# Eight output rows in one block, and single maxima in every step: a two-branch attention kernel

## The chip, the core and the metric

The kernel runs on one core of a Trainium2 chip. The metric is the device time of one execution in microseconds (us); a kernel's time is the median of its runs. The core's engines are TensorE (PE, with its weight loads PEld), VectorE (DVE), ScalarE (ACT), GpSimd (POOL) and SyncE (SP, which here only issues transfers). They run at the same time, each through its own list of instructions in order, and wait for each other by semaphores. Matmul results land in PSUM banks, which ACT and DVE read.

## The reference

Two attention branches over the same 2048 x 512 input are mixed by a gate:

```python
x = A_x
g = _sigmoid((x * gate_w).sum(-1, keepdims=True))
a = _A_ref(x, A_wqkv, A_wo)      # 32 heads of 16; each position attends to 8 earlier ones, 2 apart
b = _B_ref(x, B_wq, B_wk, B_wv, B_wo)  # 32 query heads of 16 on one key/value head, full softmax
return g * a + (1 - g) * b
```

Branch B is `softmax(q k^T / 4) v` over all 2048 keys for every one of the 32 heads, then a 512 x 512 output projection. Branch A's softmax has 8 terms a position, then its own output projection. All data is float32.

## The kernel before, in words

**Units and steps.** Branch B is cut into 32 units: 4 blocks of 512 queries by 8 groups of 4 heads (`NU`). A unit has 16 steps, one for each tile of 128 keys, so there are 512 steps (`NS`). A step s does two things on PE: `exp_pair` (L468) makes the scores of two pairs of heads in the PSUM banks `pe` (the two buffers `eb`), which ACT turns into exponentials `pexp` (L475, 128x1024 each, two a step); `weighted` (L480) multiplies the previous step's exponentials by the values and adds them into bank `po` (L483; four matmuls, eight in the profile's count). When a unit is over, `finish_a` (L495) has DVE transpose `po` (L497), after which the next unit may overwrite `po`; DVE and POOL then divide and shape the result.

**Maxima.** The softmax needs a maximum for each query and head before the exponentials of a unit start. The kernel therefore computes all scores twice: once, ahead of time, only for the maxima. A maximum task is one 62x512 matmul on one half of the array, reduced by DVE. There are 2048 of them, 64 a unit. They come in these ways:

- `fill_pair` (L339): two matmuls, one on each half of the array, into the two-bank tile `pm` (the variable `m2`); one DVE reduction (L344).
- `fill_one` (L348): one matmul into the one-bank tile `ps` (the variable `m1`), a "single"; one DVE reduction (L355).
- `fill_diff` and `fill_sum` (L411, L424): two key tiles at a time by half sums and half differences; ACT takes absolute values (L419), DVE adds and reduces (L429). Only inside the streams named below.
- `pause` (L863): when a unit's maxima would come too late, pairs are made on `pm` and on the score banks `pe`, with nothing beside them.

When the last maximum of a unit is made, `filled` (L329) has DVE reduce and transpose them, POOL splits them, and eight small transfers (L461) write them into two rows of the unit's query tile `qst`, so that the scores come out shifted. Query tiles are loaded by `stack` (L286) some units ahead; there are eight.

**The front.** `stream` (L689) makes the projections of x, matmul by matmul in halves of the array, and puts maxima beside them. It ends with the last projection in bank `pm`; near its end the list `ended` stops new pairs on `pm` (L716, L1068).

**Output rows.** The output is 16 rows of 128 positions (`NJ`). Each needs both branches' projections, three products each (high and low parts). Rows 0 to 11 are made by `out_phase` (L728), a block of four rows between two steps that again is a `stream`: output matmuls in halves (L740), row turning on PE (L646), maxima beside them. Rows 12 to 15 can only be begun when the last units are done. `spread` (L776) lays them between the last steps, up to a few matmuls at a time into `pm` (L812), with `turn_all` (L783, ACT copy L786) and `prepare` (ACT copy L637, POOL subtraction L639) for the next row; the part of the last two units (the fourth product group) is added at the very end (L1163 to L1188).

**What sets the order.** The program is a fixed list for each engine, made when it is built by the loop over steps (L1106 to L1155). That loop keeps clocks of its own (`clk`, `free`) with estimated durations, and decides with them in every step: whether an output block stands there (L1130), whether a pair is made (`fill_ready`, L853) and whether a single is made, which it is while `singles` (L849) finds more maxima left than later pairs and rows will take. `order` says in which sequence of the two score pairs, the pair and the single a step emits. Slow estimates or fast ones change the list, not the waiting on the chip.

Of the kernel before, what the change touches and what calls it, by code (L numbers as in the profile page):

```python
# [6 lines left out]
F32 = mybir.dt.float32  # L7
F32R = mybir.dt.float32r
AF = mybir.ActivationFunctionType
# [9 lines left out]
NJ = S // P  # L19
# [29 lines left out]
def gated_mix_kernel(ctx, tc, xt, wa, wk, wq, wo_a, wo_b, out):  # L49
# [36 lines left out]
    def after(eng, ready, dur):  # L86
        clk[eng] = max(clk[eng], ready) + dur
        return clk[eng]
# [219 lines left out]
        return bool(half) or bool(slots) and slots[0][0] < len(stacked) and stacked[slots[0][0]] <= clk["pe"]  # L308

    def unit_tile(v):  # L310
        for x in (v, v + 1) if pe else (v,):
            if x < NU and x not in left:
                mx[x] = wp.tile([P, 2, 2, 4, 4], F32, name="mx", bufs=3)
                if pe:
                    nc.gpsimd.memset(mx[x], -FMAX)
                    charge(250)
                else:
                    nc.scalar.activation(mx[x].rearrange("p b i t k -> p (b i t k)"), ident[:, 0:64], AF.Identity, scale=0.0, bias=mk[:, 6:7])
                left[x] = NF // NU
        return mx[v]  # L320
# [5 lines left out]
    def to_go():  # L326
        return 2 * len(slots) + len(half)
# [448 lines left out]
    def spread(js, n):  # L776

        m = 3 * (C + n)

        def turn_all(j):  # L780
            bank = m1
            for c in range(C):
                nc.tensor.transpose(bank[:, c * P:(c + 1) * P], oa[c // 2][:, j, c % 2 * P:(c % 2 + 1) * P], ident)  # L783
            after("pe", 0, 0.7)
            own = p2[0].tile([P, C, P], F32, name="raw", bufs=1)
            nc.scalar.activation(own, bank.rearrange("p (c q) -> p c q", c=C), AF.Copy)  # L786
            after("act", clk["pe"] + T_LAT, 0.6)
            return own

        def parts_a(j, own):  # L790
            nonlocal pool
            hi, lo = turned[j, 0] = [pe[0].tile([P, C, P], F32R, name=f"turned{x}", bufs=1) for x in range(2)]
            nc.scalar.activation(hi, own, AF.Copy)
            at = after("act", clk["pe"], 0.6)
            nc.gpsimd.tensor_sub(lo, own, hi.bitcast(F32))
            pool = max(pool, 1e3 * at) + 1300

        prepare(js[0], n)
        yield 1.0
        parts_a(js[0], turn_all(js[0]))  # L800
        yield 3.0
        while slots or half:
            yield 1.0
        for j in js:
            nxt = j + 1 if j != js[-1] else None
            items = []
            for i in range(m):
                items = items or out_items(j, n)
                st, mv = items[i]
                for b in range(2):  # L810
                    h = slice(64 * b, 64 * b + 64)
                    nc.tensor.matmul(m2[:, b, :], st()[h], mv[h], start=(i == 0), stop=(i == m - 1))  # L812
                after("pe", 0, T_R)
                row_left[0] = m - 1 - i
                if i == 3 * n and nxt:
                    prepare(nxt, n)
                if i == m - 8 and nxt:
                    raw = turn_all(nxt)
                if i < m - 1:
                    yield 0.0  # L820
            del turned[j, 0], turned[j, 1]
            x = len(parts)
            if x < 2:
                spare.append(p2[0].tile([P, 512], F32, name="part", tag=("own", "tr8")[x], bufs=1))
            elif x == 2:
                two = p2[0].tile([P, 2, 512], F32, name="part", tag="pr", bufs=1)
                spare.extend([two[:, 0, :], two[:, 1, :]])
            parts[j] = spare[x]
            nc.scalar.activation(parts[j], m2[:, 1, :], AF.Copy)
            after("dve", after("act", clk["pe"] + T_LAT, 0.5), 0.7)  # L830
            nc.vector.tensor_add(parts[j], m2[:, 0, :], parts[j])
            if nxt:
                parts_a(nxt, raw)
            yield 1.5
        done.add("last")

    def spread_some(k):
# [11 lines left out]
    def singles(s):  # L849

        return 2 * max(0, 16 * (NU - 1) - 16 - s) + PER_ROW * max(0, NJ - 4 - outs) < to_go()
# [208 lines left out]
    def done_mm(at):  # L1060
        nonlocal pool
        x, i = at
        lump = lumps[x]
        if i % 3 == 2:
            run_tasks()
            if p2:
                run_pool()
        if x == last - 1 and i == 3 * C - 2:  # L1068
            ended.add(1)
        if x == last and i in (2, 7):  # L1070
            exp_pair(0, int(i == 2))
        if i < 3 * C - 1:
            return
        if lump[0] == "q":
            m = lump[1]
            queries_post(m, eb[x % 2])
            free[f"e{x % 2}"] = clk["act"]
            ahead_wa(0, m - 4)
        else:
            gg, j = lump[1:]  # L1080
            a_post(gg, j, 2 if x == last else x % 2)
            if gg + 1 < C:
                ahead_wa(gg + 1, j - 2)
# [22 lines left out]
    for s in range(NS + 1):  # L1106
        u, kt = divmod(s, NJ)
        if s == 16 * NB + 4:
            half_back()
        if len(stacked) < NU and s > 16 * (home(len(stacked))[1] + 1):  # L1110
            stack(len(stacked))
        if s < NS and kt == 0 and u not in shifted:
            while u not in shifted:
                clk["pe"] += 0.5
                run_tasks()
                if u not in shifted and left.get(u, 1):
                    assert pause(4)
        v = min(x[0][0] for x in (half, slots, [(NU,)]) if x)
        need = left.get(v, NF // NU)
        steps = 16 * v - 6 - s  # L1120
        short = need - 2.8 * max(0, steps) if v < NU else 0
        lead = (NF - to_go()) / 64 - s / 16
        order = (0, "m2", "m1", 1) if s > 1 else (1, "m2", 0, "m1") if s else ()
        k, n = outs // 4, C - (outs >= NJ - 4)
        if outs == NJ - 4:
            if NU - 3 in shaped and not half and not singles(s) and not later_rows and "last" not in done:
                later_rows.append(spread(list(range(outs, NJ)), n))
            if short > 0 and steps < 2:
                pause(short)
        elif due or outs < NJ and s and kt == 0 and outs // NH in done and NHG * (k + 1) - 1 in shaped and (lead < LEAD or s >= 16 * (NHG * (k + 2) + 1)):  # L1130
            if not due:
                prepare(outs, n)
                due.append(n)
            else:
                out_phase(list(range(outs, outs + 4)), due.pop(), kt == 1)
                outs += 4
                order = (0, "m1", 2)
        elif short > 0 and steps < 2:
            pause(short)

        for which in order:
            if which == "m2":
                fill_ready("m2", M2S)
            elif which == "m1":
                if not later_rows and (kt or not s) and singles(s):
                    fill_ready("m1", M1S)
            elif s < NS:
                exp_pair(s, which % 2 or which // 2, which == 2)
        spread_some(4)
        if s:  # L1150
            weighted(s - 1)
            if kt == 0 and s < NS:
                finish_a(u - 1, nc.gpsimd)
        run_tasks()
        run_pool()  # L1155
# [10 lines left out]
    for x in range(2):  # L1166
        js = slice(2 * x, 2 * x + 2)
        two = pe[0].tile([P, 2, 256], F32, name="ttl", tag="tt", bufs=2)
        tt, own = two[:, 0].rearrange("p (b d) -> p b d", d=32), two[:, 1]
        nc.vector.transpose(two[:, 0], po[:, 256 * x:256 * x + 256])  # L1170
        rl = wp.tile([P, 8], F32, name="rll", tag="rl", bufs=2)
        nc.vector.reciprocal(rl, tt[:, :, 16])
        nc.vector.tensor_mul(rl, rl, gate_t[:, NQB - 1, js].rearrange("p j b -> p (j b)"))
        nc.vector.tensor_mul(obp["t"][:, 8 * x:8 * x + 8, 1, :], tt[:, :, 0:DH], rl.unsqueeze(2).to_broadcast([P, 8, DH]))
        nc.vector.transpose(own, obp["t"][:, 8 * x:8 * x + 8].rearrange("p b h d -> p (b h d)"))
        tl = wp.tile([P, 2, 256], F32R, name=f"tl{x}", tag="aext", bufs=2)
        nc.scalar.activation(tl[:, 0], own, AF.Copy)
        nc.gpsimd.tensor_sub(tl[:, 1], own, tl[:, 0].bitcast(F32))
        tls.append(tl)
    for x in range(2):  # L1180
        for k, w in ((0, woh), (0, wol), (1, woh)):
            for t in range(2):
# [35 lines left out]
```

## Time and profile before

| | |
|---|---|
| median of 3 runs | 1504.08 us (1503.17 to 1506.13) |
| profiled execution | 1503.76 us, its span 1502.0 us |
| granted PE clock, mean | 0.997 |
| scores and exponentials: ACT L475 | 1021 x 1.02 us |
| weighted matmuls: PE L483 | 4096, 0.61 us each, up to eight overlapped |
| pairs: DVE L344 | 508 x 1.22 us |
| singles: DVE L355 | 446 x 0.68 us |

In the profile's rows a line like L344 is the line of the kernel, `out<-in` are tile names, `x8` is a count of merged instructions, and a bracket at the end gives the idle time of that engine before it and what ended it. Rows of the timeline begin with the start in us from the span's start and then the time from the first start to the last end. Rows of a table by windows give the window, its length, then the busy time and count of PE, PEld, DVE, ACT and POOL, the granted PE clock, and the share and rate of the transfers.

### The profile page before, as it was taken

How to read it: one execution, taken by the hardware profiler on the slowest of the kernel's cores; microseconds unless marked ns; L12 is line 12 of the kernel's file. 1: busy time of each engine (PE TensorE's matmuls, PEld its weight loads, DVE VectorE, ACT ScalarE, POOL GpSimd, SP SyncE). 2: the span in 40 equal slices, each digit the busy share in tenths (PEclk: the TensorE clock that was granted, in tenths of full speed). 3: DMA queues.
4: the chain of work that ended last, by engine and by line, in shares of the span. 5: the costliest groups of instructions: out<-in, count | busy, mean ns of one | idle time of the engine just before them, and what ended most of it. 6: DMA issues, size and time to landing. Idle time of an engine off the chain costs nothing.

```text
span 1502.0 us, 29449 instructions
## 1 busy us (share of the span) xinstructions
PE 1479.2 (98%) x11020; PEld 710.5 (47%) x11020; DVE 1188.4 (79%) x1814; ACT 1285.7 (86%) x1672; POOL 1024.8 (68%) x1806
## 2 busy tenths in 40 slices
PE   9999999999999999999999999999999999999998
PEld 6899888433333333333733345333333463333343
DVE  6976666788888888888788888888888888888801
ACT  5568988899999999999899988999989889999785
POOL 7876988788888888988988799788897130111021
PEclk9999999999999999999999999999999999999999
DMA  6754223121120211211212112021120000000000
GB/s 219 212 147 143 76 87 117 33 83 46 60 84 12 73 58 41 70 41 41 69 41 70 41 41 87 12 70 41 41 76 16 12 30 12 2 1 2 1 2 28
DMA packets 44287, 87.75 MB, mean 58 GB/s; under 512 B 9520, under 2 KB 25952, under 8 KB 39920
## 3 DMA queue, kind: packets, MB, share of 16 engines
q1 hardware_dynamic: 37136, 46.89, 10.3%
q0 software_dynamic: 6432, 37.94, 7.5%
q8 instruction: 86, 1.41, 0.4%
q10 hardware_dynamic: 576, 1.05, 0.2%
q14 instruction: 57, 0.47, 0.1%
HBM read 59.02 MB, written 26.30 MB: 57 GB/s over the span
## 4 chain that ended last, share of the span: by engine, by line
PE 91%; ACT 5%; DVE 2%; issue 1%; DMA 0%; POOL 0%; SPq 0%; DVEq 0%; ACTq 0%; POOLq 0%
PE po L483 33%; PE pe L473 25%; PE pe L1057 8%; PE pm L324 8%; PE ps L324 5%; PE pe L740 4%; PE pm L409 2%; ACT dd L419 2%; ACT pexp L475 1%; PE ps L409 1%; PE pm L812 1%; PE po L409 1%; PE pe L183 1%; DMA xraw<-xt 0%; DVE mx L344 0%
## 5 line engine op out<-in xcount | busy, mean ns | idle before, releaser
L475 ACT ACTIVATE pexp<-pe 128x1024 f32<-128x1024 f32 x1021 | 987.3, 1023 | 106.0 <-PE pe L473 103.6
L344 DVE TENSOR_REDUCE mx<-pm 128x2 f32<-128x1024 f32 x508 | 620.0, 1221 | 147.4 <-PE pm L324 139.6
L483 PE MATMUL po<-pexp,vst 128*32 128x512 f32 x4096 | 546.6, 606 | 0.0
L473 PE MATMUL pe<-qst,kst 64*128 64x512 f32 x1914 | 520.4, 455 | 5.6 <-DVE mx L344 2.9
L473 PEld LDWEIGHTS pe<-qst,kst 64*128 64x128 f32 x1914 | 213.3, 184 | 424.6 <-ACT pexp L475 410.2
L355 DVE TENSOR_REDUCE mx<-ps 128x1 f32<-128x512 f32 x446 | 303.1, 680 | 2.1 <-PE ps L324 2.1
L324 PE MATMUL pm<-kst,qst 62*128 62x512 f32 x968 | 196.8, 398 | 2.9 <-DVE mx L344 2.1
L543 POOL TENSOR_TENSOR pr<-aext 128x256 f32<-128x256 f32 x256 | 182.6, 741 | 3.4 <-DMA aext<-ad 3.1
L324 PE MATMUL ps<-kst,qst 62*128 62x512 f32 x422 | 177.3, 420 | 0.5 <-DVE mx L355 0.3
L603 POOL TENSOR_TENSOR oa<-oa,av 128x256 f32<-128x256 f32 x224 | 164.5, 734 | 14.9
L483 PEld LDWEIGHTS po<-pexp,vst 128*32 128x32 f32 x4096 | 80.6, 108 | 174.5 <-issue 166.6
L600 POOL TENSOR_TENSOR av<-aext,lg 128x256 f32<-128x256 f32 x224 | 139.7, 623 | 12.5
L324 PEld LDWEIGHTS ps<-kst,qst 62*128 62x128 f32 x422 | 77.5, 184 | 68.3 <-DVE mx L355 64.9
L1057 PE MATMUL pe<-wah,xl 64*128 64x384 f32 (+1 forms) x504 | 108.9, 338 | 0.0
L419 ACT ACTIVATE dd<-pm 128x512 f32<-128x512 f32 x166 | 92.0, 608 | 19.6 <-PE pm L409 9.5
L1057 PE MATMUL pe<-wah,xh 64*128 64x384 f32 (+1 forms) x504 | 108.6, 337 | 0.0
L1057 PE MATMUL pe<-wal,xh 64*128 64x384 f32 (+1 forms) x504 | 108.3, 337 | 0.0
L429 DVE CUSTOM_DVE_ANT_0 dd<-ps,dd 128x512 f32<-128x512 f32 x83 | 57.4, 692 | 58.4 <-PE ps L409 25.4
L324 PEld LDWEIGHTS pm<-kst,qst 62*128 62x128 f32 x968 | 93.2, 187 | 8.0 <-DVE mx L344 3.4
L509 POOL TENSOR_TENSOR rl<-rl,gate_t 128x16 f32<-128x16 f32 x31 | 6.9, 222 | 118.2 <-DVE rl L503 118.1
L549 POOL TENSOR_TENSOR tr<-pr 128x512 f32<-128x512 f32 x64 | 81.7, 1277 | 4.1
L549 POOL TENSOR_TENSOR tr<-tr 128x256 f32<-128x256 f32 (+1 forms) x128 | 72.5, 567 | 9.0
(215 smaller groups left out, 1908.1 us busy)
## 6 DMA issues: line engine op xcount, KB each, us to landing
aext<-ad POOLq DMA_DIRECT2D x32, 1056.0 KB, 5.5
ad<-stage SPq DMA_DIRECT2D x32, 384.0 KB
qst<-qd SPq DMA_DIRECT2D x60, 128.0 KB
xraw<-xt SPq DMA_DIRECT2D x16, 256.0 KB
qd<-qhi SPq DMA_DIRECT2D x16, 256.0 KB
qd<-qlo SPq DMA_DIRECT2D x16, 256.0 KB
qst<-qd SPq DMA_DIRECT2D x60, 64.0 KB
qst<-ml SPq DMA_DIRECT2D x216, 2.0 KB
```

Of the source, the lines that this page charges most:

```text
L324: nc.tensor.matmul(dst, qst[home(v)[0]][b:b + 62, pr, t * P:(t + 1) * P], kst[b:b + 62, kc * 512:(kc + 1) * 512], start=True, stop=True)
L344: nc.vector.tensor_reduce(m[:, :, pr, t, kc], dst, AX.X, ALU.max)
L355: nc.vector.tensor_reduce(m[:, odd, pr, t, kc:kc + 1], dst, AX.X, ALU.max)
L419: nc.scalar.activation(dd[0][:, odd], m2[:, odd, :], AF.Abs)
L473: nc.tensor.matmul(bank[:, odd, :], kst[b:b + 64, kt * P:(kt + 1) * P], qst[home(u)[0]][b:b + 64, pr, :], start=True, stop=True)
L475: nc.scalar.activation(e, bank, AF.Exp, scale=SCALE)
L483: nc.tensor.matmul(po[32 * i:32 * i + 32, :], vst[:, kt, :], pexp[s, i // 2][:, i % 2, :], start=(kt == 0), stop=(kt == NJ - 1))
L543: nc.gpsimd.tensor_mul(pr[:, k], q, e[:, o:o + NH, AC:2 * AC])
L549: nc.gpsimd.tensor_add(nx, cur[:, :, 0:n], cur[:, :, n:2 * n])
L600: nc.gpsimd.tensor_mul(av, e[:, o:o + NH, 2 * AC:].rearrange("p j (h d) -> p j h d", d=DH), lg[:, w].unsqueeze(3).to_broadcast([P, NH, AG, ...
L603: nc.gpsimd.tensor_add(ao, ao, av)
L1057: nc.tensor.matmul(front[2 if x == last else x % 2][0][:, b, :n], l[h], r[h], start=(i == 0), stop=(i == 3 * C - 1))
```

## The change

There are seven edits. (1) `unit_tile` also takes the next unit's tile ahead in the front. (2) In `spread`, at the end of each late row but the last, DVE copies one half of `pm` and adds the other, at once, in place of an ACT copy and a DVE addition; for the last row ACT copies, and the addition moves behind the first half of the closing work. (3) The stop of pairs near the front's end comes four positions earlier. (4) The first output block takes eight rows in place of four, so there are two blocks (eight rows, then four) in place of three, and the condition for the first asks for twice as many units. (5) Late rows may begin when at most 9 maxima are left, and no longer only when no singles are wanted. (6) Singles may be placed in every step, the first of a unit (`kt == 0`) included; in that step's list the last weighted matmuls of the unit before and the transposition of `po` follow behind the single. (7) In the closing work the second half's subtraction goes from POOL to DVE.

```diff
     def unit_tile(v):
-        for x in (v, v + 1) if pe else (v,):
+        for x in (v, v + 1):
...
             parts[j] = spare[x]
-            nc.scalar.activation(parts[j], m2[:, 1, :], AF.Copy)
-            after("dve", after("act", clk["pe"] + T_LAT, 0.5), 0.7)
-            nc.vector.tensor_add(parts[j], m2[:, 0, :], parts[j])
             if nxt:
+                nc.vector.tensor_copy(parts[j], m2[:, 1, :])
+                nc.vector.tensor_add(parts[j], m2[:, 0, :], parts[j])
                 parts_a(nxt, raw)
-            yield 1.5
+                after("dve", clk["pe"] + T_LAT, 1.4)
+                yield 1.5
+            else:
+                nc.scalar.activation(parts[j], m2[:, 1, :], AF.Copy)
...
-        if x == last - 1 and i == 3 * C - 2:
+        if x == last - 1 and i == 3 * C - 6:
             ended.add(1)
...
-        k, n = outs // 4, C - (outs >= NJ - 4)
+        rows = 4 if outs else 8
+        k, n = (outs + rows) // 4 - 1, C - (outs >= NJ - 4)
         if outs == NJ - 4:
-            if NU - 3 in shaped and not half and not singles(s) and not later_rows and "last" not in done:
+            if NU - 3 in shaped and to_go() <= 9 and not later_rows and "last" not in done:
...
-                out_phase(list(range(outs, outs + 4)), due.pop(), kt == 1)
-                outs += 4
+                out_phase(list(range(outs, outs + rows)), due.pop(), kt == 1)
+                outs += rows
...
-                if not later_rows and (kt or not s) and singles(s):
+                if not later_rows and singles(s):
                     fill_ready("m1", M1S)
...
-        nc.gpsimd.tensor_sub(tl[:, 1], own, tl[:, 0].bitcast(F32))
+        (nc.vector if x else nc.gpsimd).tensor_sub(tl[:, 1], own, tl[:, 0].bitcast(F32))
         tls.append(tl)
+        if not x:
+            nc.vector.tensor_add(parts[NJ - 1], m2[:, 0, :], parts[NJ - 1])
```

Built, the changed program has the same 2048 maxima. As the two lists of instructions stand: the eight-row block is at step 272 (before: blocks of four at steps 208, 272 and 400), the four-row block at step 400 as before; the late rows run in steps 489 to 508 (before 492 to 511); DVE has 475 reductions of singles on `ps` (before 446) and 501 of pairs on `pm` (before 508); 104 matmuls on `pm` make differences in the output blocks (before 110) and none on the score banks (before five matmuls in the pause at step 488).

## The prediction

> **What bounds the kernel now.** I read the page's busy table first, then its chain, then its groups.
>
> ```profile
> span 1502.0 us, 29449 instructions
> PE 1479.2 (98%) x11020; PEld 710.5 (47%) x11020; DVE 1188.4 (79%) x1814; ACT 1285.7 (86%) x1672; POOL 1024.8 (68%) x1806
> PE 91%; ACT 5%; DVE 2%; issue 1%; DMA 0%; POOL 0%; SPq 0%; DVEq 0%; ACTq 0%; POOLq 0%
> L475 ACT ACTIVATE pexp<-pe 128x1024 f32<-128x1024 f32 x1021 | 987.3, 1023 | 106.0 <-PE pe L473 103.6
> ```
>
> PE sets the time (91% of the chain), ACT follows. A busy average cannot price this change, so I went to the timeline and cut it into slices, each from one step's weighted matmuls (L483) to the next step's. First twelve equal slices by their ends, then a stretch around the end of a unit:
>
> ```profile
> 927.90 1.06 PE L483 MATMUL po<-pexp,vst 128*32 128x512 f32 x8
> ...
> 953.77 1.06 PE L483 MATMUL po<-pexp,vst 128*32 128x512 f32 x8
> 987.69 1.07 PE L483 MATMUL po<-pexp,vst 128*32 128x512 f32 x8
> 988.47 0.68 DVE L355 TENSOR_REDUCE mx<-ps 128x1 f32<-128x512 f32 x1
> 989.31 3.80 ACT L475 ACTIVATE pexp<-pe 128x1024 f32<-128x1024 f32 x4 [0.22 <-PE pe L473]
> 989.47 1.23 DVE L344 TENSOR_REDUCE mx<-pm 128x2 f32<-128x1024 f32 x1 [0.31 <-PE pm L324]
> 989.58 1.06 PE L483 MATMUL po<-pexp,vst 128*32 128x512 f32 x8
> 990.72 0.72 DVE L497 STREAM_TRANSPOSE tt<-po 128x512 f32<-128x512 f32 x1
> 991.74 1.07 PE L483 MATMUL po<-pexp,vst 128*32 128x512 f32 x8
> ```
>
> The twelve slices (four score matmuls, a maxima pair on pm, a single on ps, the weighted matmuls) take (953.77 - 927.90) / 12 = 2.156 us. The slice 987.69 to 989.58 has the pair but no single: 1.89. There ACT runs without a pause (3.80 for four exponentials), so a slice with neither cannot be much shorter. Thus a pair in a step is nearly free, and a single costs 0.26 us for one maximum. That price decides the case.
>
> **The change, part by part.** In steps 1 to 485 (up to the tail), I count in the two programs' instruction order what each slice holds. Before: 413 with pair and single, 64 with the pair alone, 5 thinner ones, 3 blocks of four output rows. After: 433, 37, 13 thinner ones and 2 blocks, of eight rows and of four. Of the thinner ones before, 2 hold a single (2.15) and 3 do not (1.90): 10.0. Of the 13 after, 10 hold a single and half a pair (2.15) and 3 a single alone; that slice the trace lacks: between 1.90 and 2.15, and I take 1.90, because without the pair ACT is the limit. That makes 27.2. Sum: 20 x 2.156 - 27 x 1.90 + 17.2 = **+9.0 us**. Of this 2.2 is the one more ordinary step that stands where the first block stood.
>
> The blocks, by the weighted matmuls on both sides of each:
>
> ```profile
> 715.40 1.06 PE L483 MATMUL po<-pexp,vst 128*32 128x512 f32 x8
> 734.56 0.50 PE L740 MATMUL pe<-woh,own 64*128 64x512 f32 x2 [0.24 <-ACT turned L653]
> 743.62 0.73 PE L740 MATMUL pe<-woh,own 64*128 64x512 f32 x3 [0.24 <-ACT turned L653]
> 751.86 1.06 PE L483 MATMUL po<-pexp,vst 128*32 128x512 f32 x8
> 886.52 1.06 PE L483 MATMUL po<-pexp,vst 128*32 128x512 f32 x8
> 922.81 1.06 PE L483 MATMUL po<-pexp,vst 128*32 128x512 f32 x8
> 925.65 1.06 PE L483 MATMUL po<-pexp,vst 128*32 128x512 f32 x8
> 1193.97 1.06 PE L483 MATMUL po<-pexp,vst 128*32 128x512 f32 x8
> 1231.13 1.06 PE L483 MATMUL po<-pexp,vst 128*32 128x512 f32 x8
> ```
>
> Three blocks are 36.46 + 36.29 + 37.16 = 109.9 us. An inner row is 743.62 - 734.56 = 9.06 us with 20 maxima in it; there a maximum shares its PE slot with half of an output matmul, so it costs about half of a single's 0.26, 0.12 taken. Four rows more in one block hold 65 maxima instead of 80: 4 x 9.06 - 15 x 0.12 = 34.4, so the eight-row block is 36.4 + 34.4 = 70.8, the other about 36.4. Together 107.2, **-2.7**. The slice behind a block takes 925.65 - 922.81 = 2.84 instead of 2.16; one falls away, **-0.7**. Merging therefore saves little by itself: it gives 12 cheap maxima back to the steps. The moved rows take their work along: eight ACT copies, POOL's two subtractions a row, and four stores of output rows, which stood in SP's queue ahead of query loads and shifts and now follow them; no slice of before waits for one of these, so I price that at nothing; a store that came late would have to hold up a query load by the slack of a whole unit before PE saw it.
>
> At the units' ends stands a new wait. The single now placed in the last slice of a unit puts its 0.68 us reduction on DVE ahead of the transposition of po (L497), behind which queue the reciprocal, the next pair's reduction and, on PE, the next weighted matmuls, since they overwrite po. By the rows above: the pair's reduction ends at 990.70, the single's then at about 991.38, the transposition at 992.10; the weighted matmuls, 0.26 later than before by the single itself, want po at 992.00. So about 0.05 to 0.1 there, and the pair's reduction that follows ends 0.6 later, against a slack near 0.5 before PE's next pair: together 0.15 a unit. Ends: 0.04, if only po's wait shows; 0.38, if the whole 0.68 less the slack of 0.30 (991.74 - 991.44) shows. 28 units: **+4.2** (1.1 to 10.6).
>
> The front's end:
>
> ```profile
> 268.40 0.50 PE L409 MATMUL pm<-kcd,q 62*128 62x512 f32 x2
> 268.74 0.34 PE L1057 MATMUL pe<-wal,xh 64*128 64x384 f32 x2
> 270.08 0.45 PE L1057 MATMUL pm<-wah,xh 64*128 64x384 f32 x2 [0.83 <-ACT dd L419]
> ```
>
> The rule that stops the pairs earlier takes out the pair at 268.40; the last projection then no longer waits 0.83 for ACT to empty pm, and 0.34 of PE goes with the pair: about **-1.3**, after the small rest that the stage copies need (0 if ACT's copies hold it anyway, -1.6 with the two singles). The initial value of one mx tile goes from POOL to ACT: nothing, one of 64 elements among the loads.
>
> The tail holds the gain:
>
> ```profile
> 1416.45 1.06 PE L483 MATMUL po<-pexp,vst 128*32 128x512 f32 x8
> 1422.13 0.80 PE L473 MATMUL pe<-qst,kst 64*128 64x512 f32 x2 [2.90 <-DVE mx L344]
> 1423.71 1.94 PE L483 MATMUL po<-pexp,vst 128*32 128x512 f32 x8
> 1426.72 1.28 PE L483 MATMUL po<-pexp,vst 128*32 128x512 f32 x8
> 1432.76 0.49 PE L473 MATMUL pe<-qst,kst 64*128 64x512 f32 x2 [0.57 <-ACT pexp L475]
> 1455.56 0.53 ACT L637 ACTIVATE own<-ob 128x384 fp32r<-128x384 f32 x1
> 1458.16 0.60 ACT L786 ACTIVATE raw<-ps 128x512 f32<-128x512 f32 x1
> 1462.01 0.64 ACT L793 ACTIVATE turned<-raw 128x512 fp32r<-128x512 f32 x1
> 1462.17 0.69 DVE L831 TENSOR_TENSOR part<-pm,part 128x512 f32<-128x512 f32 x1 [13.81 <-ACT part L829]
> 1462.92 0.96 PE L812 MATMUL pm<-woh,own 64*128 64x512 f32 x6 [0.25 <-DVE part L831]
> 1488.68 1.07 PE L483 MATMUL po<-pexp,vst 128*32 128x512 f32 x8
> 1420.40:1427.20 6.80, 5.07 (x22) 1.74 (x26) 3.40 (x5) 2.67 (x3) 0.00 (x0) 0.50 0.00 0
> ```
>
> Before, nine maxima come in one pause that borrows the score banks: PE waits 2.90 us for DVE, and then its granted clock is 0.50 for 6.8 us. From 1416.45, two slices after step 485, to the last weighted matmuls it is 72.2 us; with those two slices 76.5. After, the same maxima go in pairs into steps 486 to 489, the first turned row overlaps them, the four rows run in steps 489 to 508 and the last three slices have only scores. I follow ACT and PE through it by these durations: 486 to 489 end after 10.5 us (ACT's 0.53, 0.60 and 0.64 copies make PE wait about 1.2), the 19 slices to 508 match 53.6 us of before, plus 0.5 because the last one now has scores, minus 3 x 0.25 for the wait on L831 (two DVE operations right at a row's end, 0.69 each, instead of an ACT copy queued behind an exponential), and the last three 5.4, by ACT's exponentials. Sum 69.3, **-7.2**. Ends: -9.5 if ACT's copies find gaps, -4.5 if they are paid twice.
>
> Beside the clock row stands a rule of the Trainium skill, "TensorE: Matmul & The Clock Gate", section "What's actually happening": an idle window of about 3.4 us drops the clock to half. The trace agrees, with an even shorter wait of 2.90 and 0.50 granted. If the shorter waits left in the tail dropped it too, that would be the last rival below; the forecast takes no drop.
>
> Behind the last weighted matmuls the fourth row's sum moves into the closing DVE chain (+0.69), that chain starts 0.3 earlier, and one subtraction goes from POOL to DVE. Two rows tell that DVE and POOL hold each other up there:
>
> ```profile
> 1492.32 0.73 POOL L1178 TENSOR_TENSOR tl<-ttl,tl 128x256 fp32r<-128x256 f32 x1 [13.73 <-ACT tl L1177]
> 1492.39 0.68 DVE L1173 TENSOR_TENSOR rll<-rll,gate_t 128x8 f32<-128x8 f32 x1
> ```
>
> The product took 0.68 under POOL's subtraction; the added sum now lies over that time. I take **0** (-0.4 to +0.4).
>
> Sum: 9.0 - 2.7 - 0.7 + 4.2 - 1.3 - 7.2 = +1.3 us on the profiled execution's 1503.76 (span 1502.0 and 1.8 around it). The median shown is 0.3 above that execution, so I forecast 1505.4 us.
>
> **The rivals.** *DVE becomes the bound at the units' ends* (slower). For it: DVE has 0.3 us of slack a slice and gets 0.68 more just where it has 0.97 of other work. Against it: the slice two steps later has no single in either kernel, so the lag is repaid. At 0.38 a unit the time is 1505.4 + 28 x 0.23 = 1511.8; it passes 0.2% from about 0.21 a unit on.
> *The lag is absorbed and the tail gives all* (faster): 0.04 a unit and -9.5 in the tail, -3.1 - 2.3 from the forecast: 1500.0. For it: no weighted matmul of before waits for L497; against it: ACT's three copies come in two slices.
> *The clock drops in the new tail again*: slices under the half clock took 1426.72 - 1423.71 = 3.01 instead of 1.90, so two of them give +2.2: 1507.6. Against it: no single wait there comes near 2.90.
> *The change leaves the pause in place*: ruled out by the order, which has no maxima on the score banks any more; two lone pairs before the scores of steps 488 and 489 remain.
>
> **How the numbers follow.** Forecast 0.42, slower at units' ends 0.28, faster 0.23, clock 0.07. What this kernel's measurement can tell from no change is about 0.2%, 3.0 us, so within is 1501.1 to 1507.1; the forecast's own range is 1501.5 to 1508. A quarter of the forecast's chance reaches above 1507.1 and a little below 1501.1. So faster 0.26, within 0.34, slower 0.40. The range 1499.5 to 1511.5 takes in both rivals' bulk.
>
> **What would show it.** Weighted-to-weighted slices with pair and single still at 2.15, 30 at units' ends gone from 1.90 to 2.15; the first weighted matmuls of a unit with a wait on L497 below 0.1; an eight-row block near 71 us; no 0.83 wait at the front's end; no half clock and no wait above 1 us around steps 486 to 490; 69 us from step 485's weighted matmuls to the last ones. Wrong it would be by waits above 0.2 a unit, or by a tail that gains under 5 or over 9 us.

## The result, and the profile after

The changed kernel takes 1509.13 us (median of 11 runs, 1506.8 to 1512.08), the kernel before, run beside it, 1504.91 (11 runs, 1503.04 to 1509.6). The ratio is 1.0028, 95% interval 1.0017 to 1.0040: slower by about 0.3%, clear of no change, and 3.7 us above the forecast. The profiled execution took 1511.71 us against 1503.76, +7.9 where the sum had +1.3.

The page after, its span, busy times, chain and first group:

```profile
span 1509.9 us, 29447 instructions
PE 1484.8 (98%) x11020; PEld 713.7 (47%) x11020; DVE 1193.5 (79%) x1827; ACT 1281.3 (85%) x1662; POOL 1024.5 (68%) x1808
PE 86%; ACT 5%; POOL 3%; DMA 2%; issue 2%; DVE 1%; SPq 1%; DVEq 0%; POOLq 0%; ACTq 0%
L475 ACT ACTIVATE pexp<-pe 128x1024 f32<-128x1024 f32 x1022 | 990.7, 1022 | 108.6 <-PE pe L473 105.3
```

The busy averages hardly moved. New in the chain are DMA (2%), SP's queue (1%) and POOL (3%): somewhere the kernel now waits for a transfer. To find the place I cut every profile at the same rows of L483: the first weighted matmuls of steps 0, 485 and 511. From them come five stages (us):

| kernel | to step 0 | 0 to 485 | of it, 75 to 80 | 485 to 511 | 511 to the end | all after step 0 |
|---|---|---|---|---|---|---|
| before | 274.24 | 1137.91 | 10.96 | 76.54 | 13.30 | 1227.75 |
| after | 276.29 | 1153.01 | 18.05 | 68.74 | 11.89 | 1233.64 |
| `after_again` | 274.34 | 1152.60 | 17.40 | 68.76 | 11.90 | 1233.27 |
| `weights_ahead` | 276.74 | 1145.95 | 11.20 | 69.13 | 11.65 | 1226.72 |
| `before_weights_ahead` | 278.76 | 1136.66 | 10.92 | 79.74 | 15.66 | 1232.07 |
| `weights_ahead_four` | 276.91 | 1151.65 | 11.21 | 66.34 | 11.65 | 1229.64 |
| `rows_later` | 280.04 | 1148.94 | 14.72 | 68.76 | 11.90 | 1229.60 |
| `before_late` | 276.17 | 1144.93 | 17.67 | 76.13 | 13.30 | 1234.37 |
| `weights_ahead_no_firsts` | 275.02 | 1139.15 | 10.95 | 72.21 | 11.90 | 1223.26 |
| `weights_ahead_pool_end` | 275.32 | 1146.45 | 11.21 | 69.11 | 13.18 | 1228.75 |
| `best_again` | 274.97 | 1139.46 | 10.97 | 71.20 | 11.91 | 1222.57 |
| `best_four` | 275.27 | 1139.27 | 10.96 | 74.08 | 11.87 | 1225.22 |
| `best_old_tail` | 274.00 | 1139.33 | 10.96 | 71.36 | 14.38 | 1225.07 |

The first column differs by 2 us between two profiles of the very same kernel (after and `after_again`) and by up to 6 in all; a part of that is spells of half clock in the front, none in `after_again`, one of 3.41 us in after and three in `rows_later`. So single profiles are compared by the last column. By it the change costs +5.9: steps +15.1, tail -7.8, close -1.4. Of the +15.1, 7.1 stand in five steps. The timeline of after at that place (bracket: idle time before the row, and what ended it; the weighted matmuls at 445.28, 453.30 and 456.87 are those of steps 78, 79 and 80):

```profile
442.14 0.59 POOL L532 DMA_DIRECT2D aext<-ad  x1
442.24 0.63 ACT L81 ACTIVATE woh<-os 128x512 fp32r<-128x512 f32 x1
442.41 2.21 SPq L625 DMA_DIRECT2D os<-wo_b  x2
442.76 1.94 ACT L475 ACTIVATE pexp<-pe 128x1024 f32<-128x1024 f32 x2
445.28 1.07 PE L483 MATMUL po<-pexp,vst 128*32 128x512 f32 x8
449.70 0.63 ACT L81 ACTIVATE woh<-os 128x512 fp32r<-128x512 f32 x1 [5.00 <-DMA os<-wo_b]
450.24 2.98 ACT L475 ACTIVATE pexp<-pe 128x1024 f32<-128x1024 f32 x3
451.30 0.80 PE L473 MATMUL pe<-qst,kst 64*128 64x512 f32 x2 [4.95 <-ACT pexp L475]
453.30 1.94 PE L483 MATMUL po<-pexp,vst 128*32 128x512 f32 x8
456.87 1.07 PE L483 MATMUL po<-pexp,vst 128*32 128x512 f32 x8
```

And the same place in the timeline of before:

```profile
432.75 5.30 SPq L461 DMA_DIRECT2D qst<-ml  x8
438.15 2.74 SPq L625 DMA_DIRECT2D os<-wo_b  x2
438.60 0.59 POOL L532 DMA_DIRECT2D aext<-ad  x1
440.78 0.63 ACT L81 ACTIVATE woh<-os 128x512 fp32r<-128x512 f32 x1
441.31 2.84 ACT L475 ACTIVATE pexp<-pe 128x1024 f32<-128x1024 f32 x3
```

A piece of branch B's output weights (`wo_b`, 256 KB, L625) is loaded by SP; ACT splits it (L81) a step or two later, and in ACT's list the exponentials stand behind that split. Beside it POOL loads branch A's next tile (L532, 1 MB). Before, the weights are issued 0.45 us ahead of that load, and at 440.78 ACT takes them without a wait, 2.6 us after the issue. After, they are issued 0.27 behind it, and land 7.27 us after their issue, as the chain of waits has it:

```profile
441.69 0.61 SPq L461
...
442.41 7.27 DMA os<-wo_b
...
450.24 1.01 ACT pexp L475
```

ACT waits 5.00 us and PE 4.95. PE's granted clock is 0.50 for 6.83 us, from 3.3 us into that wait until 456.47. The windows from 430 to 460, before and after (window, length, busy time and count of PE, PEld, DVE, ACT and POOL, granted clock, share and rate of the transfers):

```profile
430.00:460.00 30.00, 29.82 (x210) 10.55 (x208) 25.14 (x28) 27.91 (x30) 27.22 (x48) 1.00 0.22 69
```

```profile
430.00:460.00 30.00, 25.05 (x161) 9.10 (x160) 20.14 (x25) 21.57 (x24) 21.68 (x35) 0.89 0.26 78
```

The Trainium skill says in "TensorE: Matmul & The Clock Gate", section "What's actually happening", that an idle window of about 3.4 us halves the clock; the wait of 4.95 and the clock of 0.89 agree.

Both loads stand in the same steps of the two programs' lists; what moved is time. Counted from step 0, SP issues the load of the weights 163.9 us on before and 166.1 after: it stands behind eight shift transfers (L461), and those wait for POOL. Most of these 2.2 us is no lateness against the work around it, for step 75 itself begins 160.7 us on before and 162.5 after, and ACT comes to the split 1.9 us later too. POOL's 1 MB load moved from 164.4 to 165.9. So the weights fell back by 0.3 us against the step that needs them and by 0.7 against the 1 MB load, which was enough to put them behind it. POOL's rows show where the 0.7 comes from: the last parts of the shifts (L446, L447) come one product of branch A (L600, 0.62 us) later in POOL's order, before behind an L603,

```profile
431.46 0.73 POOL L603 TENSOR_TENSOR oa<-oa,av 128x256 f32<-128x256 f32 x1
432.16 0.24 POOL L446 TENSOR_TENSOR mt<-mt,mk 128x32 f32<-128x32 f32 x1
```

after behind the L600 that follows it:

```profile
435.83 0.62 POOL L600 TENSOR_TENSOR av<-aext,lg 128x256 f32<-128x256 f32 x1
436.41 0.24 POOL L446 TENSOR_TENSOR mt<-mt,mk 128x32 f32<-128x32 f32 x1
```

The tail shows what the prediction said: no row of PE has a wait above 0.42 us between 1425 and 1445, and the granted clock is 1.00.

```profile
1425.00:1445.00 20.00, 19.57 (x143) 7.77 (x146) 10.46 (x12) 17.20 (x21) 5.27 (x9) 1.00 0.01 2
```

### The profile page after: what moved, and what is told of

The parts are those of the page before. It is cut to its first block, busy times and chain, and to the rows that moved or that the text cites. A ratio compares the mean times of both kernels' runs of the same rounds, so it can differ in the third digit from the quotient of the medians.

```text
span 1509.9 us, 29447 instructions
## 1 busy us (share of the span) xinstructions
PE 1484.8 (98%) x11020; PEld 713.7 (47%) x11020; DVE 1193.5 (79%) x1827; ACT 1281.3 (85%) x1662; POOL 1024.5 (68%) x1808
## 4 chain that ended last, share of the span: by engine, by line
PE 86%; ACT 5%; POOL 3%; DMA 2%; issue 2%; DVE 1%; SPq 1%; DVEq 0%; POOLq 0%; ACTq 0%
PE po L483 32%; PE pe L473 25%; PE pm L324 8%; PE pe L1059 7%; PE ps L324 4%; PE pe L740 3%; PE pm L409 2%; PE pm L812 1%; ACT dd L419 1%; ACT pexp L475 1%; PE ps L409 1%; DMA ad<-stage 1%; PE po L409 1%; DMA os<-wo_b 0%; PE pe L183 0%
## 5 line engine op out<-in xcount | busy, mean ns | idle before, releaser
L344 DVE TENSOR_REDUCE mx<-pm 128x2 f32<-128x1024 f32 x501 | 612.1, 1222 | 151.1 <-PE pm L324 149.1
L483 PE MATMUL po<-pexp,vst 128*32 128x512 f32 x4096 | 546.4, 605 | 0.3 <-ACT pexp L475 0.3
L473 PE MATMUL pe<-qst,kst 64*128 64x512 f32 x1916 | 533.3, 454 | 7.6 <-ACT pexp L475 7.4
L473 PEld LDWEIGHTS pe<-qst,kst 64*128 64x128 f32 x1916 | 219.8, 184 | 413.6 <-ACT pexp L475 405.8
L355 DVE TENSOR_REDUCE mx<-ps 128x1 f32<-128x512 f32 x475 | 322.8, 679 | 3.7 <-PE ps L324 3.7
L324 PE MATMUL ps<-kst,qst 62*128 62x512 f32 x449 | 189.9, 423 | 0.3 <-DVE mx L355 0.3
L603 POOL TENSOR_TENSOR oa<-oa,av 128x256 f32<-128x256 f32 x224 | 164.2, 733 | 14.9
L483 PEld LDWEIGHTS po<-pexp,vst 128*32 128x32 f32 x4096 | 80.6, 108 | 184.8 <-issue 173.0
L600 POOL TENSOR_TENSOR av<-aext,lg 128x256 f32<-128x256 f32 x224 | 139.4, 622 | 12.9
L324 PEld LDWEIGHTS ps<-kst,qst 62*128 62x128 f32 x449 | 82.7, 184 | 76.7 <-DVE mx L355 73.9
L324 PEld LDWEIGHTS pm<-kst,qst 62*128 62x128 f32 x958 | 94.5, 187 | 10.5 <-DVE mx L344 5.6
```

Of the source, the lines that this page charges most:

```text
L324: nc.tensor.matmul(dst, qst[home(v)[0]][b:b + 62, pr, t * P:(t + 1) * P], kst[b:b + 62, kc * 512:(kc + 1) * 512], start=True, stop=True)
L344: nc.vector.tensor_reduce(m[:, :, pr, t, kc], dst, AX.X, ALU.max)
L355: nc.vector.tensor_reduce(m[:, odd, pr, t, kc:kc + 1], dst, AX.X, ALU.max)
L473: nc.tensor.matmul(bank[:, odd, :], kst[b:b + 64, kt * P:(kt + 1) * P], qst[home(u)[0]][b:b + 64, pr, :], start=True, stop=True)
L483: nc.tensor.matmul(po[32 * i:32 * i + 32, :], vst[:, kt, :], pexp[s, i // 2][:, i % 2, :], start=(kt == 0), stop=(kt == NJ - 1))
L600: nc.gpsimd.tensor_mul(av, e[:, o:o + NH, 2 * AC:].rearrange("p j (h d) -> p j h d", d=DH), lg[:, w].unsqueeze(3).to_broadcast([P, NH, AG, ...
```

## The experiments

Two theories stood at the start. *Late weights*: the load behind the shifts meets the 1 MB load, and that is why the kernel is slower. *Singles*: the added maxima at the units' first steps cost more than the tail gives, and the stall at step 79 is a chance event of one execution. All times are medians, beside runs of the kernel before on the same chip:

| kernel | us (range) | ratio to before, 95% interval |
|---|---|---|
| `after_again` | 1510.58 (1508.73 to 1513.62) | 1.0031 (1.0020 to 1.0042) |
| `weights_ahead` | 1504.62 (1502.82 to 1505.97) | 0.9986 (0.9976 to 0.9995) |
| `before_weights_ahead` | 1511.04 (1507.14 to 1512.61) | 1.0027 (1.0017 to 1.0038) |
| `weights_ahead_four` | 1508.08 (1504.99 to 1511.41) | 1.0010 (0.9998 to 1.0022) |
| `rows_later` | 1508.22 (1506.66 to 1511.42) | 1.0017 (1.0008 to 1.0025) |
| `before_late` | 1510.88 (1509.18 to 1516.31) | 1.0039 (1.0026 to 1.0053) |
| `weights_ahead_no_firsts` | 1501.57 (1499.53 to 1503.77) | 0.9972 (0.9961 to 0.9983) |
| `weights_ahead_pool_end` | 1506.93 (1503.80 to 1509.23) | 1.0002 (0.9990 to 1.0014) |
| `best_again` | 1501.24 (1499.32 to 1504.92) | 0.9968 (0.9956 to 0.9980) |
| `best_four` | 1502.80 (1500.04 to 1504.22) | 0.9967 (0.9954 to 0.9979) |
| `best_old_tail` | 1501.93 (1500.30 to 1505.07) | 0.9970 (0.9961 to 0.9980) |

The kernel before had 1506.74 us beside the first four of them, 1505.64 beside the next four and 1506.65 beside the last three.

**The change once more.** `after_again` is the changed kernel itself.

> The changed kernel once more, unaltered, for a second profile. Theory (late weights): the slice in step 79 that took 8.0 us is made by the program's order, because the load of a part of wo_b is issued behind eight shift transfers and just behind the 1 MB load of branch A's rows, and ACT's split of it stands ahead of the exponentials. Then a second profile shows a wait of ACT for that load again, 3 to 6 us, and the median is 1509 +- 1.5. Rival (chance of that one execution): the slice is 2.15 us, no wait of ACT for a load, and the profiled execution is near 1507 while the median stays near 1509 for another reason.

ACT waited 4.06 us for the same load, and the slices of steps 79 and 80 took 7.06 and 3.87 us, where they took 8.02 and 3.56 in the first profile. So the stall is no accident of one execution.

**The weights further ahead.** `weights_ahead` loads two pieces together and splits them at the next such place of the list, some 60 us later, so that a late landing no longer stands in front of an exponential:

```diff
-    for i in range(2 * C + 1):
-        wos.append([(wo_load, kcs[i])] if i < 2 * C else [])
-        wos[-1] += [(wo_split, kcs[i - 1])] if i else []
+    for i in range(0, 2 * C + 1, 2):
+        wos.append([(wo_split, x) for x in kcs[max(0, i - 2):i]])
+        wos.append([(wo_load, x) for x in kcs[i:i + 2]])
```

> The changed kernel with each part of the output weights loaded one round of branch A's work (some 25 steps) ahead of its split, two parts at a time, so that no split can wait for its load. Late weights: 5 to 7 us less than the changed kernel, 1502.5 to 1504.5, and no slice above 3.2 us between steps 2 and 200. Rival (singles at the units' ends are the loss, 28 places): 1508 to 1510, as the changed kernel.

The windows from 430 to 460 of this kernel:

```profile
430.00:460.00 30.00, 29.84 (x208) 10.52 (x206) 25.31 (x32) 27.77 (x30) 27.24 (x51) 1.00 0.26 86
```

PE is as busy as before the change, the five steps take 11.20, and the time falls by 6.0 us against `after_again`, to just under the kernel before.

**The same edit on the kernel before.** If late weights are what the change brought, the edit should leave the kernel before alone.

> The kernel before with the same earlier loads. Late weights: the kernel before waits for no such load in its profile, so 1505 +- 1.2, no gain beyond 1 us (two splits in one step cost ACT some tenths). Rival (earlier loads help for another reason, such as a quieter queue): 2 us or more below the kernel before.

It was slower, and not by its loads: the steps took 1136.66, 1.3 less. But the moved loads shifted the estimated clocks of the list, the first block came at step 224 in place of 208, and in the pause ten maxima fell to the score banks in place of five. The timeline of PE in that pause:

```profile
1422.61 0.49 PE L324 MATMUL pe<-kst,qst 62*128 62x512 f32 x2 [0.93 <-DVE mx L344]
...
1429.40 0.80 PE L473 MATMUL pe<-qst,kst 64*128 64x512 f32 x2 [1.47 <-DVE mx L344]
```

The tail took 79.74 and the close 15.66. A control on a list that rearranges itself is no control; `before_late` below replaces it.

**Blocks of four.** `weights_ahead_four` is `weights_ahead` with three blocks:

```diff
-        rows = 4 if outs else 8
+        rows = 4
```

> As the changed kernel with weights ahead, but with three output blocks of four rows instead of one of eight and one of four. By the prediction's terms the merged block is worth 2.7 + 0.7 - 2.2 = 1.2 us and the 8 to 10 maxima it gives up cost 0.26 each in steps, so nearly nothing in sum: within 1.5 us of the kernel with weights ahead. Rival (merging is the loss): 2 to 4 us faster than it. Rival (merging is the gain): 2 to 4 us slower than it.

After step 0 it takes 2.9 us more (blocks 109.9 against 106.0), and 3.5 by the medians: outside the expected 1.5, as the rival had it by which merging is the gain. Here the late rows already begin in step 485, so the border between steps and tail lies elsewhere and only the sum compares.

**The 1 MB load later.** `rows_later` moves one statement of POOL behind the pieces of weights; it was meant to move nothing else:

```diff
-            yield from load(i + 3)
             for _ in range(2):
                 if p2b and extra:
...
+            yield from load(i + 3)
```

> The changed kernel with one edit in POOL's work alone: the 1 MB load of branch A's rows is issued behind the two turns of output weights instead of ahead of them. The list of PE's instructions is the same to the last one. Late weights: the weights' load no longer stands behind the 1 MB, the slice in step 79 goes from 7 or 8 us to 2.2 and the one after from 3.6 to 2.2: 5 to 7 us less than the changed kernel, 1503 to 1506. Rival (the eight shift transfers ahead of it in SP's queue make it late, not the 1 MB): the wait stays, 1509 to 1511.

Its timeline, SP, ACT, PE and POOL:

```profile
440.38 5.30 SPq L461 DMA_DIRECT2D qst<-ml  x8
445.61 0.63 ACT L81 ACTIVATE woh<-os 128x512 fp32r<-128x512 f32 x1
445.78 2.20 SPq L625 DMA_DIRECT2D os<-wo_b  x2
448.34 0.63 ACT L81 ACTIVATE woh<-os 128x512 fp32r<-128x512 f32 x1 [2.10 <-DMA os<-wo_b]
449.93 0.50 PE L473 MATMUL pe<-qst,kst 64*128 64x512 f32 x2 [2.35 <-ACT pexp L475]
450.25 0.59 POOL L532 DMA_DIRECT2D aext<-ad  x1
```

Alone, the weights land 2.56 us after their issue, not 7.27, yet ACT still waits 2.10, the five steps take 14.72, and the expected 1503 to 1506 was missed (by the ratios it is about 2 us faster than `after_again`). But the edit moved more than the 1 MB load. In after, two exponentials stand in ACT's list between the split at 442.24 and the one that waits; here the second split stands right behind the first, at 445.61. ACT asks for the weights one step earlier, 166.2 us after step 0 and not 168.4. So this run doesn't part the late issue from the load beside it. An estimate from these rows can: issued 166.1 after step 0 as in after, and landing 2.56 later, the weights would be there at 168.7, and ACT, asking at 168.4, would wait 0.3 us in place of 5.00. By that the neighbour is nearly all of the wait; no run here has shown it with the split in its old place.

**The stall put into the kernel before.** `before_late` adds two transfers of 2 KB ahead of this one load of the kernel before, into scratch that nobody reads:

```diff
+    spot = [dp.tile([16, 32], F32, name=f"spot{x}") for x in range(2)]
...
+        if (k, c) == (1, 0):
+            for x in range(2):
+                nc.sync.dma_start(spot[x], ident[0:16, 0:32])
```

> The kernel before with two extra transfers of 2 KB to a spare place in SP's queue, ahead of the one load of weights that was late in the changed kernel; nothing else differs. That issues the load about 1.2 us later, 0.8 behind the 1 MB load instead of 0.4 ahead of it. Late weights: a wait of ACT for the load of 4 to 6 us in step 79 and a half clock, 5 to 7 us slower than the kernel before. Rival (the wait needs the changed order of the steps): within 1 us of the kernel before.

Its timeline (lines are one to four higher by the inserted ones):

```profile
440.05 1.12 SPq L628 DMA_DIRECT2D spot<-ident  x2
440.52 0.59 POOL L533 DMA_DIRECT2D aext<-ad  x1
441.27 1.53 SPq L629 DMA_DIRECT2D os<-wo_b  x2
447.47 0.63 ACT L82 ACTIVATE woh<-os 128x512 fp32r<-128x512 f32 x1 [4.69 <-DMA os<-wo_b]
```

Two tiny transfers of 1.12 us in SP's queue cost the kernel before 5.2 us by the medians (1510.88 against 1505.64): the weights now follow the 1 MB load by 0.75, land 6.2 us after their issue, ACT waits 4.69, and the five steps take 17.67. This shows with none of the change's seven edits in the kernel that an issue 1.2 us later is enough for the stall. By the estimate above the weights alone would have made ACT wait about 1.1 of the 4.69.

**No singles at the units' first steps.** `weights_ahead_no_firsts` puts edit (6) back:

```diff
-                if not later_rows and singles(s):
+                if not later_rows and (kt or not s) and singles(s):
```

> As the changed kernel with weights ahead, but no singles at the units' first steps (the condition of before). It leaves out no maximum: those that are not made there come elsewhere, 3 of them in a pause at the end. The prediction's term: 28 singles at 0.26 and a wait of 0.09 to 0.15 a unit go, 7.3 + 2.5 to 4.2 us, and about as many singles must be paid for elsewhere or in a pause of 3 to 7 us. Theory (the units' ends are cheap and the singles only trade places with the pause): 1503 to 1507, within 2 us of weights ahead. Rival (DVE's lag at the units' ends is the loss): 3 us or more faster than weights ahead, 1501 or below.

Steps -6.8, tail +3.1, against `weights_ahead`; together -3.5, and -3.1 by the medians. 447 singles are left of 472. So the singles at the first steps buy 3.1 us of tail with 6.8 us of steps. It beats both kernels. The expected range, within 2 us of `weights_ahead`, was missed: the gain has the size that the rival named, though not by its cause alone, for the last slices of the units went from 2.15 back to 1.90, and the lag was the smaller part (2.01 back to 1.92 in the units' second slices).

**The last subtraction back on POOL.** `weights_ahead_pool_end` puts edit (7) back:

```diff
-        (nc.vector if x else nc.gpsimd).tensor_sub(tl[:, 1], own, tl[:, 0].bitcast(F32))
+        nc.gpsimd.tensor_sub(tl[:, 1], own, tl[:, 0].bitcast(F32))
```

> As the changed kernel with weights ahead, but with the last subtraction of the closing work on POOL, as before. In the profiles of before POOL's last wait for its own end lasts 6.8 us from that subtraction's start and is over 1.6 us after SP's; in those of after it is over before SP's. Theory (POOL's end set the program's end): 1.2 to 1.5 us slower than weights ahead, and 13.2 +- 0.3 us from the last weighted matmuls to the end instead of 11.7. Rival (the subtraction is hidden): within 0.3 us and 11.7.

The close took 13.18 against 11.65, as expected (the ratios differ by 0.0016, about 2.4 us, with wide intervals). The reason is in the sequencers' own records at the program's end, which the page doesn't count as busy (engine, instruction, start and duration in us):

```
before   GpSimd DRAIN 1494.37  6.83    Sync DRAIN 1499.68    GpSimd barrier 1501.25
after    GpSimd DRAIN 1501.43  7.15    Sync DRAIN 1509.15    GpSimd barrier 1509.18
```

GpSimd's closing DRAIN starts with its last subtraction and takes some 7 us. Before, it ended 1.57 us behind SP's and set the end; after, that subtraction is the first half's and the DRAIN is over before SP's.

**The best version again, and two parts of the change in it.** `best_again` is `weights_ahead_no_firsts`; `best_four` has three blocks of four in it; `best_old_tail` has the old ends of the late rows, their old condition, and the last sum ahead of the closing work.

> The kernel with weights ahead and no singles at the units' first steps, unaltered, beside the kernel before and the two variants below. It should again be 3 to 5 us faster than the kernel before (ratio 0.9965 to 0.998). If it is within 1.5 us of it, the earlier gain was the front's chance.

> As best_again, but with three output blocks of four rows. Theory (each block costs one fixed edge and the rows themselves cost the same): blocks and the slices behind them 1.2 to 3.5 us more than best_again, as with weights_ahead_four. Rival (merging is worth nothing, the 3.5 us there were its late start of the tail): within 1 us of best_again from the first to the last weighted matmuls.

> As best_again, but with the late rows as before: ACT copies and DVE adds at each row's end, the late rows begin only when no singles are wanted, and the last sum stands ahead of the closing work. The closing subtraction stays on DVE. By the prediction the three waits of 0.25 us come back and the late rows start later: 1 to 4 us more than best_again, all of it behind step 485. Rival (the tail's gain came only from the missing pause): within 1 us.

Three blocks of four take the same time in the steps (1139.27 against 1139.46). In the tail they cost 2.9 in this profile, which neither expectation had: in the pause five maxima fall to the score banks instead of three. PE's timeline there, first `best_four`, then `best_again`:

```profile
1424.53 0.50 PE L473 MATMUL pe<-qst,kst 64*128 64x512 f32 x2 [2.90 <-DVE mx L344]
1425.73 1.93 PE L483 MATMUL po<-pexp,vst 128*32 128x512 f32 x8
```

```profile
1423.00 0.49 PE L473 MATMUL pe<-qst,kst 64*128 64x512 f32 x2 [1.77 <-DVE mx L344]
1424.01 1.07 PE L483 MATMUL po<-pexp,vst 128*32 128x512 f32 x8
```

After the wait of 2.90 the weighted matmuls take 1.93 (half clock), after 1.77 they take 1.07. The second is not the rule, though: in `weights_ahead_no_firsts`, an earlier profile of this same kernel, the half clock came after the same wait:

```profile
1422.74 0.50 PE L473 MATMUL pe<-qst,kst 64*128 64x512 f32 x2 [1.77 <-DVE mx L344]
1423.75 1.63 PE L483 MATMUL po<-pexp,vst 128*32 128x512 f32 x8
```

Its tail took 72.21 in place of 71.20, so about 1 of the 2.9 us is whether the clock fell, and that differs between executions of one kernel. The medians differ by 1.6 us, but the two ratios are 0.9967 and 0.9968: the worth of merging, if any, lies in the tail and below what the runs can tell. `best_old_tail` loses 2.5 us in the close, where the last matmuls of the late rows, ACT's copy and the last sum lie ahead of the DVE chain, and the product on DVE takes 0.68 instead of 0.17. The late rows themselves, where the expectation looked for the loss, took the same (71.36 against 71.20), beside a pause with a shorter wait (1.16 against 1.77). Its median is 0.7 above `best_again`, which the runs cannot tell from none.

## Why the prediction was wrong where it was

The time, 1509.13, lies in the range of 1499.5 to 1511.5, but 1.1 above the forecast's own range; "slower", the sign with the largest chance (0.40), came true, though not by the rival that carried most of it. That both held is luck in good part. After step 0 the prediction had +2.6 (its sum without the front) and the profile +5.9: a stall of 7.1 that was in no term, less 1.9 in the blocks, 1.4 in the close and 0.6 in the tail. By its steps:

**The step that failed** is the sentence on the queues, with the moved stores and what stands in SP's queue: "no slice of before waits for one of these, so I price that at nothing; a store that came late would have to hold up a query load by the slack of a whole unit before PE saw it". I looked only for what was moved past the query loads and took a slack of a whole unit for all of SP's queue. The load of the weights has no such slack: before, ACT takes it 2.63 us after its issue, and alone it lands after 2.56 (`rows_later`). In that queue it stands behind transfers that wait for POOL. The edits moved it by 0.3 us against its step and by 0.7 against the 1 MB load, behind which it now fell, and it cost +7.1, with none of the seven edits touching it. `before_late` and `weights_ahead` show from both sides that the late landing makes the stall. That the 1 MB load beside it makes most of the lateness is an estimate. Of the 1.9 us by which step 75 comes later, the slices at the four unit ends ahead of it, where edit (6) puts singles, make up 1.4. Why the list puts the shifts one product later on POOL was not tried.

**Steps 1 to 485 by their form, and the units' ends.** Predicted +9.0 - 0.7 + 4.2 = +12.5; measured, the rest without blocks and stall, 15.1 + 4.6 - 7.1 = +12.6. The price of a single was right: the last slice of a unit grew from 1.90 to 2.17, the mean over the units without the one of the stall. The lag at the units' ends was nearly right in kind and too large: the first slice stayed at 2.15, so the wait for L497 costs nothing, and the second grew from 1.91 to 2.02 (slices behind blocks left out), 0.11 a unit and not 0.15. That the sum fits to 0.1 hides misses that cancel: the slices by their form came to about +9.9 and not +9.0, the lag to 3.1 and not 4.2, the slices behind blocks to -0.4 and not -0.7. The timeline of one unit's end in after, PE, then DVE:

```profile
1004.02 1.07 PE L483 MATMUL po<-pexp,vst 128*32 128x512 f32 x8
1006.13 1.06 PE L483 MATMUL po<-pexp,vst 128*32 128x512 f32 x8
1007.46 0.50 PE L324 MATMUL pm<-kst,qst 62*128 62x512 f32 x2
1008.12 1.07 PE L483 MATMUL po<-pexp,vst 128*32 128x512 f32 x8
```

```profile
1004.73 0.68 DVE L355 TENSOR_REDUCE mx<-ps 128x1 f32<-128x512 f32 x1
1005.33 0.70 DVE L497 STREAM_TRANSPOSE tt<-po 128x512 f32<-128x512 f32 x1
1006.24 1.16 DVE L344 TENSOR_REDUCE mx<-pm 128x2 f32<-128x1024 f32 x1
```

The transposition is over at 1006.03, just ahead of the weighted matmuls at 1006.13; the pair's reduction ends at 1007.40, and PE's next pair starts at 1007.46, right behind it. That is the lag of 0.6 against a slack near 0.5 of the prediction. The rival *DVE becomes the bound at the units' ends* is out at 0.11. Yet the singles there do cost more than they bring, by `weights_ahead_no_firsts` 3.5 us, and most of it by the plain price of 0.26 each: I had added the terms of edit (6) and of the tail without setting them against each other.

**The blocks.** Predicted -2.7; measured -4.6, a term mis-sized, by which of its parts was not looked into. The weighted matmuls on both sides in after:

```profile
867.46 1.06 PE L483 MATMUL po<-pexp,vst 128*32 128x512 f32 x8
936.57 1.06 PE L483 MATMUL po<-pexp,vst 128*32 128x512 f32 x8
...
1209.97 1.06 PE L483 MATMUL po<-pexp,vst 128*32 128x512 f32 x8
1246.15 1.06 PE L483 MATMUL po<-pexp,vst 128*32 128x512 f32 x8
```

The block of eight takes 69.11 us where I had 70.8, that of four 36.18. The conclusion beside it, that merging saves little by itself, held with edit (6) undone: `best_four` takes the same time in the steps. With edit (6), `weights_ahead_four` was 3.5 us slower by the medians.

**The tail.** Predicted 69.3 and -7.2; measured 68.74 and -7.8. Steps 486 to 489 end 10.4 us after step 485 (10.5 predicted), the last three slices take 5.42 (5.4), and no pause, no half clock is left. The rival of the clock dropping in the tail is out here. The prediction read the 2.90 us wait and the half clock of before as agreeing with the 3.4 us of the Trainium skill; they don't quite, for the clock fell at 1420.4, when PE had waited 1.2 us.

**The front's end.** The wait of 0.83 is gone, as predicted; -1.3 cannot be told in a stage that varies by 6 us.

**The close.** Predicted 0; measured -1.4. I followed DVE and PE there, and they did come to nothing: SP's last wait ends 11.0 us behind the last weighted matmuls before and 11.1 after. What set the end before was POOL's drain.

In the steps, the forecast of +9.8 (9.0 - 2.7 - 0.7 + 4.2), with -1.9 for the blocks, +0.1 for the rest and +7.1 for the stall, gives the measured +15.1; with -7.8 in the tail and -1.4 in the close that is +5.9 after step 0. Without it the change gives -1.0 (`weights_ahead` against before, 1226.72 - 1227.75) and, without edit (6) as well, -5.2 (`best_again`), which the runs confirm with 0.32% (interval 0.20% to 0.44%).

## What to carry to other kernels

A kernel with fixed lists can lose several us at a place that the change doesn't touch: when an edit shifts one queue against another by a microsecond or less, look for every transfer that a busy engine needs within one step, and price it by the wait it would cause if it came late, not by the waits that it causes now. Work put into every slot that is free by a list's rule is not free: set what it saves at the end against its price in each slot, here 6.8 us of steps for 3.1 us of tail. A control that changes the input of a scheduler has to be checked for what the scheduler moved, in the list of every engine: `before_weights_ahead` moved a block, `rows_later` a split on ACT.

## What was not expected of the hardware

- A 256 KB load issued 0.27 us behind a 1 MB load of POOL landed after 7.27 us, one issued 0.75 behind it after 6.2, one with no such neighbour after 2.56.
- GpSimd's DRAIN at the program's end took 6.83 and 7.15 us from its last instruction, and so can set the end of a kernel in which POOL works until late.
- PE's half clock came after a wait of 2.35 us (`rows_later`, granted clock 0.94 from 430 to 460), after 2.90 (`best_four`), 1.2 us into a wait of 2.90 (before), and after 1.77 in one of two profiles of the same kernel (`weights_ahead_no_firsts`, not `best_again`). So no length of wait marks the border in these runs. All are shorter than the 3.4 us of the Trainium skill's page named above; here the measurement decides. The row of `rows_later`:

```profile
430.00:460.00 30.00, 27.65 (x184) 9.60 (x180) 22.64 (x29) 24.37 (x27) 22.19 (x39) 0.94 0.36 105
```
